# A rewritten prologue: four weight pieces on a second DMA queue, weight conversion begun earlier, one conversion tick a step

## The chip, the cores and the metric

The kernel runs on one core of one Trainium2 chip. The core has TensorE (PE, matmuls, with PEld for its weight loads), VectorE (DVE), ScalarE (ACT), GpSimd (POOL) and SyncE (SP), which here only issues DMAs. The metric is the device time of one execution in microseconds (us), lower is better. The time before is 1602.67 us, the median of three runs (1602.57 to 1602.93).

## The reference

Three stages follow one another on fp32 data: an attention through 32 memory slots for each of 8 batches and 8 heads of 576 rows, a two-layer network with a leaky ReLU, and a gated network.

```python
a   = softmax(phi, axis=m)                      # (B, H, S, 32)
k_m = einsum('bhsm,bhsd->bhmd', a, k);  v_m = einsum('bhsm,bhsd->bhmd', a, v)
x   = softmax(q @ k_m.T / sqrt(64)) @ v_m       # -> (4608, 512)
h   = x @ w_in;  x = maximum(0.01*h, h) @ w_out             # 512 -> 2048 -> 512
out = (sigmoid(x @ w_gate) * (x @ w_val)) @ w2_out          # 512 -> 1536 -> 512
```

The weights `w_in`, `w_out` and those of the gated network reach the kernel as 64-bit floats; the kernel reads them as pairs of 32-bit words and turns them into fp32 on the chip.

## The kernel before, in words

**Precision.** Every large matmul is done as three matmuls in a rounded fp32 format: high times high, low times high, high times low. `split` (L185) makes the high part with an ACT cast (L186) and the low part with a subtraction (L187) on DVE or POOL.

**Units.** A unit is one batch and one group of four heads; `units[0]` and `units[1]` are the two of batch 0. A unit goes through the parts `v1` to `v11` (vector work) and `t1` to `t8` (PE work): the softmax over phi (`v1`, `t1`, `v2`, `t2`, `v3`, exponential `v3e`, `v4`), the products with k and v (`t4`, into `ps_kv`), normalising and laying out (`v5r`, `v5x`, `t5`, `v6`), q transposed (`t7a`, `v7a`, `t7b`, `v7b`), scores (`t8a`, `v8a`, `t8b`, `v8b`), the second softmax (`v9`, `v9e`, `v10`), a transpose back (`v10t`) and the split into `at_hi` and `at_lo` (`v11`). In the text, `v9.1` is part v9 of unit 1. PSUM results of these parts share the two buffers of `ps_a`; the phi tile `ph` has one buffer, so that the load of unit 1's phi is issued after unit 0's `v3` has read it.

**Weight pieces.** `w_in` and `w_out` come in 32 pieces of 512 KB (class `Piece`, L197), two of each for every one of eight column blocks. `load` issues a DMA on SP's queue. The conversion of one piece has five stages: `a`, three ACT passes over 512 elements (L214, L215, L222); `b`, one DVE pass (L226); `b2`, one DVE pass (L234); `c`, one POOL pass (L242); `d`, for a `w_out` piece, a split into high and low part. `y`, the intermediate of `a`, `b` and `b2`, lies in SBUF. `tick()` (L1122) advances a pipeline by one: at tick n it emits `a` of piece n-1, `b` of n-2, `b2` of n-3, `c` of n-4, `d` of n-5; 37 ticks convert everything.

**Order.** Every engine works in program order, and so does SP's queue. The order is written out by hand. `SCHED['loads']` is the order of the loads on SP's queue: p, k and q of a unit number, or a count of weight pieces. `SCHED['prologue']` is a list of groups; in a group, the vector parts of each unit and the ticks (`T`) are interleaved by `run` (L1113), one instruction of each in turn, and then the PE parts follow. After the prologue, `first_vw` (L1176) multiplies v_m of batch 0 with a block of `w_in` (`vw_block`, L760), which gives `vw`.

**Main loop.** A step (L1254) takes 128 columns of the 2048 and half of a batch's 576 rows: `m1_in` (L801, 6 matmuls into `ps_h`, then leaky ReLU to `gr` and a split into `gh`, `gl`) runs two steps ahead; `m1_out` (L824) adds 12 matmuls into the four PSUM banks `acc`. Batch 0 has 32 steps in four groups of four columns for either half; when a group closes, the four banks are copied or added to `obuf` or `pbuf` (L844, L842), and the next group needs the banks again. In each of the first 30 steps `SCHED['ticks']` gives the number of ticks; `done_until` (L1151) adds ticks where a weight would be late, in `step_in` (L1171) and in `first_vw`. `SCHED['vw0']` are the steps at which the other six `vw` blocks are made. From step 32 on (batch 1) nothing of this remains.

Of the kernel before, what the change touches and what calls it, by code (L numbers as in the profile page):

```python
# [19 lines left out]

SCHED = {'vw0': [2, 5, 8, 13, 20, 22],
# [5 lines left out]
 'ticks': [1, 1, 1, 1, 2, 1, 1, 2, 0, 1, 0, 1, 1, 2, 0, 0, 0, 1, 1, 1, 1, 1, 0, 0, 1, 0, 0, 0, 0, 0],  # L27
 'lopool': [0, 1, 2, 3, 4, 5, 6, 7, 8, 9, 10, 11, 12, 13, 14],
 'gldve': [3, 4, 6, 12, 26, 31],
 'upool': ['v10.1', 'v10.2', 'v10.3', 'v11.0', 'v11.1', 'v11.2', 'v11.3', 'v9.0', 'v9.2', 'v9.3'],  # L30
 'chain': {'lp': -8,
# [64 lines left out]
            'lq3': 2,  # L96
            'v1': -5,
            't1': -1,
            'v2': 0,
            't2': 1,  # L100
            'v3': 3,
# [17 lines left out]
def tile_kernel(  # L119
# [77 lines left out]
    class Piece:  # L197
        late = False

        def __init__(self, src, done, f_dst=None, raw=None):  # L200
            self.src, self.done, self.f_dst, self.raw = src, done, f_dst, raw

        def load(self):
            self.raw = self.raw() if self.raw else cvp.tile([P, 2 * PC], U32, tag="raw", name="raw", bufs=2)
            r = self.raw
            if len(self.src.shape) == 3:
                r = r.rearrange("p (c f) -> p c f", c=self.src.shape[1])
            nc.sync.dma_start(out=r, in_=self.src)

        def a(self):  # L210
            w = self.raw.rearrange("p (n t) -> p n t", t=2)
            self.y = cvp.tile([P, PC], F32, tag="y", name="y", bufs=5)
            self.k = cvp.tile([P, PC], F32, tag="k", name="k", bufs=4)
            nc.scalar.activation(self.y, w[:, :, 1].bitcast(F32), AF.Abs, scale=2.0 ** -3)  # L214
            nc.scalar.activation(self.k, w[:, :, 0], AF.Copy, scale=2.0 ** -27, bias=2.0 ** 25)  # L215
            if not self.late:
                self.sign()
            yield
# [12 lines left out]
        def b2(self):  # L231
            w = self.raw.rearrange("p (n t) -> p n t", t=2)
            yi = self.y.bitcast(I32)
            nc.vector.scalar_tensor_tensor(  # L234
                out=yi, in0=yi, scalar=3, in1=w[:, :, 1].bitcast(I32),
                op0=ALU.logical_shift_left, op1=ALU.bitwise_xor,
            )
            yield
# [317 lines left out]
    def v5r(u):  # L556
# [6 lines left out]
        yield  # L563
        if u[0] == 0:
            nc.vector.tensor_scalar_mul(r, mask, r[:, 0:1])
            yield

    def v5x(u):
        s = un[u]
        p, r = s.pop("p"), s["r"]  # L570
        x = etile(u)
        x = s["x"] = x.rearrange("p a m -> p (a m)")[:, 0:4 * D].rearrange("p (a f) -> p a f", a=2)
# [103 lines left out]
    def v9m(u):  # L676
        s = un[u]
        nb = S // 32
        st = s["st"] = ap_.tile([P, nb], F32, tag="st", name="st", bufs=2)
        nc.vector.reduce_max(st, s["sc"], axis=AX.X)  # L680
        yield
# [406 lines left out]
    with tc.manual_schedule():  # L1088
# [10 lines left out]
        for j in range(NVB):  # L1099
            pieces += win_pieces(j) + wout_pieces(j)  # L1100
        n_start = len(pieces)

        raws = iter(pieces)

        def load_raws(n):
            for _ in range(n):
                p = next(raws, None)
                if p:
                    p.load()

# [59 lines left out]

        def step_in(b, hf, fc):  # L1171
            if (b, hf) == (0, 0):
                done_until(2 * (fc - fc % 2) + 4)
            return m1_in(b, hf, fc)

        def first_vw(j):  # L1176
            done_until(4 * j + 2)
            return vw_block(j)
# [15 lines left out]
        for x in SCHED["loads"]:  # L1194
            if isinstance(x, int):
                load_raws(x)
            elif "." in x:
                unit_qh(units[int(x[1])], int(x[3]))
# [5 lines left out]
        for group in SCHED["prologue"]:  # L1204
            vs, ts_ = {}, []
            for n, f in enumerate(waiting):
                vs["w", n] = [f()]
            waiting = []
            for x in group.split():
# [4 lines left out]
                else:  # L1214
# [4 lines left out]
                    else:  # L1219
                        ts_.append((PARTS[n], u))  # L1220
            run([chain(v) for v in vs.values()])
            for t in ts_:
# [9 lines left out]
        for i in range(LA):  # L1232
            fin = step_in(*steps[i])
            if i + 1 < LA:
                fin()
# [18 lines left out]
        for i, (b, hf, fc) in enumerate(steps):  # L1254
# [3 lines left out]
            if i + LA < len(steps):  # L1258
                fin = step_in(*steps[i + LA])
            else:  # L1260
# [22 lines left out]
            for n in {b, b + 1} - {0}:  # L1283
                if i in VW_AT.get(n, []):
                    vw_pair(n, 2 * VW_AT[n].index(i))
            m1_out(b, hf, fc)
            for f, u in ls:
# [71 lines left out]
```

## Time and profile before

| | us |
|---|---|
| median of 3 runs | 1602.67 |
| profiled execution, its own time | 1601.75 |
| span of its trace, first to last instruction | 1599.9 |
| PE busy (share of the span) | 1549.1 (97%) |
| ACT / DVE / POOL busy | 707.9 / 827.7 / 431.0 |

The profile describes one execution, 0.9 us below the median; 1.85 us of its time lie outside the span. Start times are counted from the first instruction. A row of the timeline gives start, duration, engine, line, operation, the tiles (out<-in) with their shapes, a count where neighbours were merged, and in brackets the idle time of that engine just before with what ended it. PEclk is the granted clock of TensorE as a share of 2.4 GHz; 0.50 is its lower level.

### The profile page before, as it was taken

What the parts mean: (1) busy time and instruction counts of PE and PEld (TensorE: products, weight loads), DVE (VectorE), ACT (ScalarE), POOL (GpSimd) and SP (SyncE); (2) the same over time, 40 slices, a digit from 0 to 9 for tenths busy, and PEclk for the clock granted to TensorE, in tenths of its full rate; (3) what the DMA queues carried; (4) which work ended last, traced back from release to release, by engine and by line L of the source; (5) the groups of instructions that cost most, each with busy time, mean ns of one, the idle gap of its engine ahead of it and who ended that gap; (6) DMA issues with size and microseconds to landing.
All of it is one profiled execution on the core that took longest, in us unless ns stands there. A gap on an engine that the chain in (4) does not pass through costs nothing.

```text
span 1599.9 us, 27447 instructions
## 1 busy us (share of the span) xinstructions
PE 1549.1 (97%) x10544; PEld 1358.0 (85%) x10544; DVE 827.7 (52%) x1426; ACT 707.9 (44%) x1602; POOL 431.0 (27%) x429
## 2 busy tenths in 40 slices
PE   5799999999999999999999999999999999999998
PEld 2677988999999998999988888888888888888898
DVE  6886444555554545422145474355545475255544
ACT  5885455565556555645333143223333143223332
POOL 3886343554445444543100020000200020000100
PEclk8799999999999999999999999999999999999999
DMA  9822554554556455322446446536546446536692
GB/s 306 277 53 64 160 143 138 150 154 139 159 146 192 140 160 146 115 82 97 146 170 218 140 156 234 191 115 222 195 163 222 141 150 236 169 109 223 223 398 76
DMA packets 203490, 268.66 MB, mean 168 GB/s; under 512 B 95072, under 2 KB 140128, under 8 KB 203360
## 3 DMA queue, kind: packets, MB, share of 16 engines
q1 hardware_dynamic: 203360, 266.92, 52.1%
q8 instruction: 83, 1.36, 0.4%
q14 instruction: 47, 0.39, 0.1%
HBM read 219.68 MB, written 47.19 MB: 167 GB/s over the span
## 4 chain that ended last, share of the span: by engine, by line
PE 82%; ACT 1%; DVE 1%; DMA 1%; issue 0%; POOL 0%; DVEq 0%; SPq 0%; ACTq 0%; POOLq 0%
PE acc L835 20%; PE oacc L1041 18%; PE ps_y L943 14%; PE ps_h L813 9%; PE ps_x L943 9%; PE ps_z L943 9%; PE ps_vw L783 1%; PE ps_kv L550 1%; DMA wt<-gvs 1%; PE ps_sc L625 0%; ACT gr L818 0%; ACT obuf L844 0%; DVE vw L795 0%; DVE t L530 0%; ACT raw L222 0%
## 5 line engine op out<-in xcount | busy, mean ns | idle before, releaser
L835 PE MATMUL acc<-gh,wo 128*128 128x288 f32 x2048 | 428.7, 301 | 3.7 <-ACT obuf L844 2.7
L835 PEld LDWEIGHTS acc<-gh,wo 128*128 128x128 f32 x2048 | 328.9, 189 | 28.4 <-issue 13.8
L835 PE MATMUL acc<-gl,wo 128*128 128x288 f32 x1024 | 304.8, 298 | 2.1 <-POOL gl L187 2.1
L187 POOL TENSOR_TENSOR gl<-gr,gh 128x288 fp32r<-128x288 f32 x250 | 215.6, 864 | 329.9 <-ACT gh L186 216.6
L1041 PE MATMUL oacc<-w2t,pt 128*128 128x512 f32 x1296 | 296.3, 389 | 0.0
L1041 PEld LDWEIGHTS oacc<-w2t,pt 128*128 128x128 f32 x1296 | 243.1, 188 | 50.3
L943 PE MATMUL ps_y<-xo,wt 128*128 128x512 f32 (+1 forms) x1080 | 251.9, 369 | 0.0
L813 PE MATMUL ps_h<-at_hi,vw 128*128 128x288 f32 x1024 | 214.6, 298 | 6.1 <-ACT vw L186 4.7
L943 PEld LDWEIGHTS ps_y<-xo,wt 128*128 128x128 f32 x1080 | 190.4, 188 | 33.8
L818 ACT ACTIVATE gr<-ps_h 128x288 f32<-128x288 f32 x256 | 105.7, 413 | 254.2 <-PE ps_h L813 226.1
L906 POOL TENSOR_TENSOR xo<-xr,xo 128x512 fp32r<-128x512 f32 (+1 forms) x16 | 23.0, 1460 | 671.0 <-ACT xo L902 671.0
L835 PEld LDWEIGHTS acc<-gl,wo 128*128 128x128 f32 x1024 | 193.7, 189 | 3.0 <-POOL gl L187 3.0
L813 PEld LDWEIGHTS ps_h<-at_hi,vw 128*128 128x128 f32 x1024 | 166.6, 190 | 7.5 <-ACT vw L186 5.6
L943 PE MATMUL ps_z<-xo,wt 128*128 128x512 f32 (+1 forms) x720 | 167.4, 368 | 0.6 <-DMA wt<-gvs 0.6
L943 PE MATMUL ps_x<-xo,wt 128*128 128x512 f32 (+1 forms) x720 | 167.5, 368 | 0.0
L813 PE MATMUL ps_h<-at_lo,vw 128*128 128x288 f32 x512 | 151.6, 296 | 0.0
L978 ACT CAST pt<-sg 128x512 fp32r<-128x512 f32 (+1 forms) x120 | 69.4, 578 | 182.0 <-DVE sg L971 182.0
L943 PEld LDWEIGHTS ps_z<-xo,wt 128*128 128x128 f32 x720 | 127.0, 189 | 23.1 <-DVE tmp L1024 0.7
L943 PEld LDWEIGHTS ps_x<-xo,wt 128*128 128x128 f32 x720 | 127.2, 188 | 22.9
L186 ACT CAST gh<-gr 128x288 fp32r<-128x288 f32 x256 | 111.8, 437 | 2.2
L813 PEld LDWEIGHTS ps_h<-at_lo,vw 128*128 128x128 f32 x512 | 97.2, 190 | 0.0
L990 ACT COPY tmp<-ps_x 128x512 f32<-128x512 f32 (+1 forms) x60 | 32.5, 542 | 136.6 <-PE ps_x L943 136.6
(171 smaller groups left out, 1719.0 us busy)
## 6 DMA issues: line engine op xcount, KB each, us to landing
wt<-gvs SPq DMA_DIRECT2D x210, 512.0 KB, 4.6
w2t<-w2s SPq DMA_DIRECT2D x60, 512.0 KB, 5.5
gvs<-hl SPq DMA_DIRECT2D x84, 256.0 KB, 2.4
x2s<-obuf SPq DMA_DIRECT2D x15, 576.0 KB, 3.7
win<-in_moe_w_in_dram SPq DMA_DIRECT2D x16, 512.0 KB, 9.8
wo_bits<-in_moe_w_out_dram SPq DMA_DIRECT2D x16, 512.0 KB, 10.4
xr<-x2s SPq DMA_DIRECT2D x16, 512.0 KB, 6.2
out_dram<-osum SPq DMA_DIRECT2D x32, 256.0 KB, 2.0
```

The lines of the kernel that those rows point to most:

```text
L186: nc.scalar.copy(hi, raw)
L187: eng.tensor_sub(lo, raw, f32(hi))
L550: nc.tensor.matmul(p[M * h:M * h + M, 0:2 * D], a, x, start=(c == 0), stop=(c == CC))
L783: nc.tensor.matmul(ps[g][M * h:M * h + M, n * VB:(n + 1) * VB], kvT[b, g][D * g:D * g + D, 1, M * h:M * h + M], win[j][D * g:D * g + D, h, ...
L813: nc.tensor.matmul(p[:, :HALF], w, x, start=(n == 0), stop=(n == 3 * NG - 1))
L818: nc.scalar.activation(gr, p[:, :HALF], AF.Prelu, alpha=0.01)
L835: nc.tensor.matmul(a[d][:, :HALF], w[:, ds_], x, start=(open_ and n == 0), stop=(close and n == 2),)
L906: eng.tensor_sub(t[:, 1, :h], x_operand(n, k, a), f32(t[:, 0, :h]))
L943: nc.tensor.matmul(bank, w[:, l, a, :], x[:, r, :h], start=(start and i == 0), stop=(i == 5), skip_group_check=not start,)
L978: nc.scalar.copy(d[:, 0, :h], s)
L990: read(lambda: nc.scalar.copy(s1, x))
L1041: nc.tensor.matmul(bank[i], pt[2 * f + t][:, l, q * P:(q + 1) * P], w2t[f][:, r, :], start=(f == 0 and l + r == 0), stop=(f == TH - 1 and ...
```

## The change

The first four weight pieces (`a4`) are issued on ACT's queue, ahead of everything else that ACT does; on SP's queue unit 0's and unit 1's k now come before their q, and the pieces that stood between them go behind unit 1's q. The prologue's groups are rewritten: the second tick, the first that converts anything, stands with `v3e.0`; both prologues have 12 ticks. `W` in a group makes the first two `vw` blocks inside the prologue, and their `waiting` splits come after the other vector work of the next group. `v1` of unit 2 moves from the prologue to step 0, and its `t1`, `v2`, `t2` one step on. The loop's ticks become one a step at most but for one step, two `vw` blocks come two steps later and one four, one one step later, and `done_until` moves from `m1_in` to `m1_out` with a later due time. The first nine pieces keep `y` between `a` and `b2` in a PSUM bank of the `acc` pool. `r` times `mask` (L565) goes from DVE to ACT. `v10.0` goes from DVE to POOL and `v10.1` from POOL to DVE; the row maxima and sums of unit 1 lie in a PSUM bank of `ps_h`.

```diff
@@ -18,16 +18,17 @@
 
 
 
-SCHED = {'vw0': [2, 5, 8, 13, 20, 22],
- 'loads': ['p0', 'q0', 'k0', 1, 'p1', 1, 'k1', 'q1', 2, 'p2', 16, 'k2', 32, 'q2.0', 'q2.1', 'q2.2', 'q2.3'],
- 'prologue': ['v1.0', 't1.0', 'v2.0 t7a.0 t2.0', 'v7a.0 v3.0', 'v3e.0 v4.0', 't7b.0 v1.1', 'T t4.0 t1.1', 'T',
-              'v5.0', 'v7b.0', 'v2.1', 't5.0', 'v6.0 t2.1 t8a.0', 'T v3.1', 'v3e.1 v8a.0 t8b.0', 't7a.1', 'v8b.0',
-              'v9.0 v7a.1 T v4.1 v9e.0 t4.1', 't7b.1 T', 't5.1 v5.1 v7b.1', 'T v1.2', 'v10.0 T', 't8a.1 v6.1',
-              'v10t.0 t8b.1 T v8a.1', 'v11.0', 'v8b.1 v9.1 T', 'T T v9e.1 T v10.1 v10t.1 v11.1'],
- 'ticks': [1, 1, 1, 1, 2, 1, 1, 2, 0, 1, 0, 1, 1, 2, 0, 0, 0, 1, 1, 1, 1, 1, 0, 0, 1, 0, 0, 0, 0, 0],
+SCHED = {'vw0': [4, 6, 12, 14, 20, 22],
+ 'loads': ['a4', 'p0', 'k0', 'q0', 'p1', 'k1', 'q1', 16, 'p2', 'k2', 32, 'q2.0', 'q2.1', 'q2.2', 'q2.3'],
+ 'prologue': ['T v1.0', 't1.0', 'v2.0 t2.0', 'v3.0 t7a.0', 'v3e.0 T v7a.0 v4.0 t4.0 t7b.0', 'T v7b.0 v1.1 t1.1',
+              'v5.0 v2.1 t5.0 t2.1', 'v6.0 T v3.1 t8a.0', 'v3e.1 T v8a.0 t8b.0 t7a.1',
+              'v8b.0 v7a.1 v4.1 T t4.1 t7b.1', 'v9.0 v7b.1 T', 'v5.1 v9e.0 T t5.1', 'v6.1 T t8a.1 W',
+              'v8a.1 v10.0 t8b.1', 'v8b.1 v9.1 T', 'v9e.1 T v10t.0 v11.0', 'v10.1 T W', 'v10t.1 v11.1'],
+ 'ticks': [1, 1, 1, 1, 1, 1, 1, 1, 0, 1, 1, 1, 1, 1, 1, 0, 1, 1, 1, 1, 1, 2, 1, 0, 1, 1, 1, 0, 0, 0],
+ 'banks': 9,
  'lopool': [0, 1, 2, 3, 4, 5, 6, 7, 8, 9, 10, 11, 12, 13, 14],
  'gldve': [3, 4, 6, 12, 26, 31],
- 'upool': ['v10.1', 'v10.2', 'v10.3', 'v11.0', 'v11.1', 'v11.2', 'v11.3', 'v9.0', 'v9.2', 'v9.3'],
+ 'upool': ['v10.0', 'v10.2', 'v10.3', 'v11.0', 'v11.1', 'v11.2', 'v11.3', 'v9.0', 'v9.2', 'v9.3'],
  'chain': {'lp': -8,
            'lk': -5,
            'lq0': -8,
@@ -94,10 +95,10 @@
             'lq1': 0,
             'lq2': 1,
             'lq3': 2,
-            'v1': -5,
-            't1': -1,
-            'v2': 0,
-            't2': 1,
+            'v1': -1,
+            't1': 0,
+            'v2': 1,
+            't2': 2,
             'v3': 3,
             'v3e': 3,
             'v4': 4,
@@ -195,21 +196,24 @@
     PC = 512
 
     class Piece:
-        late = False
+        late = bank = False
 
         def __init__(self, src, done, f_dst=None, raw=None):
             self.src, self.done, self.f_dst, self.raw = src, done, f_dst, raw
 
-        def load(self):
+        def load(self, eng=nc.sync):
             self.raw = self.raw() if self.raw else cvp.tile([P, 2 * PC], U32, tag="raw", name="raw", bufs=2)
             r = self.raw
             if len(self.src.shape) == 3:
                 r = r.rearrange("p (c f) -> p c f", c=self.src.shape[1])
-            nc.sync.dma_start(out=r, in_=self.src)
+            eng.dma_start(out=r, in_=self.src)
 
         def a(self):
             w = self.raw.rearrange("p (n t) -> p n t", t=2)
-            self.y = cvp.tile([P, PC], F32, tag="y", name="y", bufs=5)
+            if self.bank:
+                self.y = ps_acc.tile([P, PC], F32, tag="acc", name="y_bank")
+            else:
+                self.y = cvp.tile([P, PC], F32, tag="y", name="y", bufs=5)
             self.k = cvp.tile([P, PC], F32, tag="k", name="k", bufs=4)
             nc.scalar.activation(self.y, w[:, :, 1].bitcast(F32), AF.Abs, scale=2.0 ** -3)
             nc.scalar.activation(self.k, w[:, :, 0], AF.Copy, scale=2.0 ** -27, bias=2.0 ** 25)
@@ -230,9 +234,11 @@
 
         def b2(self):
             w = self.raw.rearrange("p (n t) -> p n t", t=2)
-            yi = self.y.bitcast(I32)
+            y = self.y
+            if self.bank:
+                self.y = cvp.tile([P, PC], F32, tag="y", name="y", bufs=5)
             nc.vector.scalar_tensor_tensor(
-                out=yi, in0=yi, scalar=3, in1=w[:, :, 1].bitcast(I32),
+                out=self.y.bitcast(I32), in0=y.bitcast(I32), scalar=3, in1=w[:, :, 1].bitcast(I32),
                 op0=ALU.logical_shift_left, op1=ALU.bitwise_xor,
             )
             yield
@@ -561,13 +567,13 @@
         yield
         nc.vector.reciprocal(r[:, 0:1], r[:, 0:1])
         yield
+
+    def v5x(u):
+        s = un[u]
+        p, r = s.pop("p"), s["r"]
         if u[0] == 0:
-            nc.vector.tensor_scalar_mul(r, mask, r[:, 0:1])
-            yield
-
-    def v5x(u):
-        s = un[u]
-        p, r = s.pop("p"), s["r"]
+            r = ap_.tile([P, 4], F32, tag="r", name="r", bufs=2)
+            nc.scalar.activation(r, mask, AF.Copy, scale=s["r"][:, 0:1])
         x = etile(u)
         x = s["x"] = x.rearrange("p a m -> p (a m)")[:, 0:4 * D].rearrange("p (a f) -> p a f", a=2)
         if u[0] == 0:
@@ -676,7 +682,10 @@
     def v9m(u):
         s = un[u]
         nb = S // 32
-        st = s["st"] = ap_.tile([P, nb], F32, tag="st", name="st", bufs=2)
+        if u == FIRST2:
+            st = s["st"] = ps_h.tile([P, 512], F32, tag="h", name="st_bank")[:, :nb]
+        else:
+            st = s["st"] = ap_.tile([P, nb], F32, tag="st", name="st", bufs=2)
         nc.vector.reduce_max(st, s["sc"], axis=AX.X)
         yield
 
@@ -1099,14 +1108,16 @@
         for j in range(NVB):
             pieces += win_pieces(j) + wout_pieces(j)
         n_start = len(pieces)
+        for p in pieces[:SCHED["banks"]]:
+            p.bank = True
 
         raws = iter(pieces)
 
-        def load_raws(n):
+        def load_raws(n, eng=nc.sync):
             for _ in range(n):
                 p = next(raws, None)
                 if p:
-                    p.load()
+                    p.load(eng)
 
         STAGES = ((1, "a"), (4, "c"), (2, "b"), (3, "b2"), (5, "d"))
 
@@ -1168,13 +1179,9 @@
         steps += [(b, hf, fc) for b in range(1, B) for hf in range(2) for fc in range(NF)]
         LA = 2
 
-        def step_in(b, hf, fc):
-            if (b, hf) == (0, 0):
-                done_until(2 * (fc - fc % 2) + 4)
-            return m1_in(b, hf, fc)
-
         def first_vw(j):
-            done_until(4 * j + 2)
+            while pos[0] < 4 * j + 6:
+                run([tick()])
             return vw_block(j)
 
         def unit_parts(i):
@@ -1194,6 +1201,8 @@
         for x in SCHED["loads"]:
             if isinstance(x, int):
                 load_raws(x)
+            elif x[0] == "a":
+                load_raws(int(x[1:]), nc.scalar)
             elif "." in x:
                 unit_qh(units[int(x[1])], int(x[3]))
             else:
@@ -1203,9 +1212,6 @@
         fin = None
         for group in SCHED["prologue"]:
             vs, ts_ = {}, []
-            for n, f in enumerate(waiting):
-                vs["w", n] = [f()]
-            waiting = []
             for x in group.split():
                 if x == "T":
                     vs.setdefault("T", []).append(tick())
@@ -1218,6 +1224,9 @@
                         vs.setdefault(u, []).append(PARTS[n](u))
                     else:
                         ts_.append((PARTS[n], u))
+            for n, f in enumerate(waiting):
+                vs["w", n] = [f()]
+            waiting = []
             run([chain(v) for v in vs.values()])
             for t in ts_:
                 if t:
@@ -1230,7 +1239,7 @@
             run([first_vw(n_vw)()])
             n_vw += 1
         for i in range(LA):
-            fin = step_in(*steps[i])
+            fin = m1_in(*steps[i])
             if i + 1 < LA:
                 fin()
 
@@ -1256,7 +1265,7 @@
                 fin()
                 fin = None
             if i + LA < len(steps):
-                fin = step_in(*steps[i + LA])
+                fin = m1_in(*steps[i + LA])
             else:
                 if not tmps:
                     tmp_open()
@@ -1283,6 +1292,8 @@
             for n in {b, b + 1} - {0}:
                 if i in VW_AT.get(n, []):
                     vw_pair(n, 2 * VW_AT[n].index(i))
+            if b == 0:
+                done_until(4 * (fc // 2) + 3 + fc % 2)
             m1_out(b, hf, fc)
             for f, u in ls:
                 f(u)
```

## Rows read from the trace of the kernel before

**Rows 1.** The page's part 1, busy time, share of the span, instructions.
```profile
PE 1549.1 (97%) x10544; PEld 1358.0 (85%) x10544; DVE 827.7 (52%) x1426; ACT 707.9 (44%) x1602; POOL 431.0 (27%) x429
```

**Rows 2.** Busy time by stretch; last three columns: PEclk, DMA share, GB/s.
```profile
0.00:5.00 5.00, 0.00 (x0) 0.00 (x0) 1.70 (x9) 1.28 (x1) 0.70 (x6) 1.00 0.49 119
5.00:10.00 5.00, 3.45 (x11) 1.98 (x11) 2.27 (x6) 1.42 (x3) 0.00 (x0) 1.00 0.96 250
...
25.00:50.00 25.00, 9.42 (x66) 3.27 (x58) 24.76 (x39) 20.38 (x41) 17.59 (x15) 0.64 1.05 381
...
70.00:80.00 10.00, 9.80 (x60) 8.47 (x61) 9.24 (x11) 9.74 (x23) 8.73 (x7) 0.69 0.32 63
...
110.00:120.00 10.00, 8.79 (x62) 8.33 (x63) 9.09 (x16) 7.38 (x17) 9.92 (x10) 1.00 0.10 28
...
140.00:200.00 60.00, 59.35 (x589) 54.31 (x576) 30.90 (x70) 28.78 (x77) 25.41 (x28) 1.00 0.43 122
```

**Rows 3.** Timeline of PE in the prologue.
```profile
8.85 1.08 PE L644 MATMUL ps_qT<-ident,q 128*128 128x128 f32 x4 [1.06 <-DVE pht L518]
11.88 1.94 PE L550 MATMUL ps_kv<-kv,e 128*32 128x128 f32 x32 [1.94 <-issue]
...
14.32 0.59 PE L552 MATMUL ps_kv<-ones,t 128*128 128x2 f32 x2
...
33.43 1.23 PE L661 MATMUL ps_sc<-qT,kvT 128*64 128x288 f32 x4 [2.97 <-ACT kvT L607]
...
36.20 1.94 PE L764 MATMUL ps_vw<-win,kvT 128*32 128x256 f32 x16
...
50.79 0.61 PE L813 MATMUL ps_h<-at_hi,vw 128*128 128x288 f32 x1 [4.72 <-ACT vw L186]
```

**Rows 4.** Timeline of ACT in the prologue and the first steps.
```profile
16.54 0.52 ACT L575 ACTIVATE e<-ps_kv,r 128x64 f32<-128x64 f32 x2 [1.30 <-DVE r L565]
...
53.70 0.41 ACT L818 ACTIVATE gr<-ps_h 128x288 f32<-128x288 f32 x1 [2.48 <-PE ps_h L813]
...
55.98 0.68 ACT L214 ACTIVATE y<-wo_bits 128x512 f32<-128x512 f32 x1
56.55 0.67 ACT L215 ACTIVATE k<-wo_bits 128x512 f32<-128x512 uint32 x1
...
69.77 1.28 ACT L844 COPY obuf<-acc 128x288 f32<-128x288 f32 x4
```

**Rows 5.** DVE's groups, shapes apart, 0 to 55 us: count, busy us, mean ns.
```profile
L226 DVE TENSOR_SCALAR y<-y 128x512 f32<-128x512 f32 x11 | 8.8, 799 | 0.0
L234 DVE SCALAR_TENSOR_TENSOR y<-y,win 128x512 int32<-128x512 int32 x6 | 6.4, 1060 | 0.0
...
L565 DVE TENSOR_SCALAR r<-mask,r 128x4 f32<-128x4 f32 x2 | 1.1, 548 | 0.1
...
L530 DVE TENSOR_REDUCE t<-e 128x128 f32<-128x512 f32 x1 | 1.0, 1032 | 0.5 <-ACT e L523 0.5
L671 DVE STREAM_TRANSPOSE e<-ps_sc 128x288 f32<-128x288 f32 x2 | 1.0, 483 | 0.9 <-PE ps_sc L661 0.8
...
L687 DVE TENSOR_TENSOR unit_a<-unit_a,st 128x576 f32<-128x576 f32 x1 | 0.7, 747 | 0.0
...
L516 DVE TENSOR_TENSOR e<-ph,ps_m 128x512 f32<-128x512 f32 x1 | 0.7, 687 | 1.5 <-PE ps_m L501 1.5
...
L518 DVE TENSOR_TENSOR pht<-pht,ps_m 64x128 f32<-64x128 f32 x1 | 0.3, 274 | 0.0
```

**Rows 6.** Timeline of PE: a block of vw, and the first matmul of step 4.
```profile
61.28 1.19 PE L764 MATMUL ps_vw<-win,kvT 128*32 128x256 f32 x16
...
70.20 0.85 PE L835 MATMUL acc<-gh,wo 128*128 128x288 f32 x2 [2.73 <-ACT obuf L844]
```

**Rows 7.** PE's waits from 50 to 140 us: total, times, longest.
```profile
PE acc L835 <- ACT obuf L844: 2.7, 1, 2.7
PE acc L835 <- POOL gl L187: 2.1, 3, 1.1
```

More of the change, by code (lines that the diff above doesn't have):

```diff
@@ L563, in v5r @@
         yield
-        if u[0] == 0:
-            nc.vector.tensor_scalar_mul(r, mask, r[:, 0:1])
-            yield
     def v5x(u):
@@ L570, in v5x @@
         p, r = s.pop("p"), s["r"]
+        if u[0] == 0:
+            r = ap_.tile([P, 4], F32, tag="r", name="r", bufs=2)
+            nc.scalar.activation(r, mask, AF.Copy, scale=s["r"][:, 0:1])
         x = etile(u)
```

## The prediction, made before the change was run

> **What bounds the kernel now.** I read the page's part 1 first: PE is busy for 97% of the span [rows 1], so only time in which PE stands idle or slow can be won. The table by stretch says where that is. From 140 us on PE is busy 59.35 of 60 us [rows 2], and the edits touch batch 0 alone, whose 32 steps end near there. Before 50 us PE has almost nothing to do; the first matmul of the main loop starts at 50.79 us [rows 3]. So two places count: the prologue, judged by the first `gr`, at 53.70 us [rows 4], and the 32 steps behind it.
>
> In the prologue DVE is busy for 24.76 of the 25 us from 25 to 50, but only for 4 of the first 10 us, and ACT for 2.7 [rows 2]. That is the room which an earlier conversion could use. In the steps the list of PE's waits is short: the longest is 2.73 us on the copies into `obuf`, at step 4, and three on `gl` sum to 2.1 us [rows 6, 7]. Behind the long one PEclk is 0.69 for ten microseconds [rows 2]: (1 - 0.69) x 10 = 3.1 us of PE lost, more than the wait itself. The wait of 1.1 us that is the longest on `gl` [rows 7] falls between 100 and 120 us, and the stretch from 110 keeps 1.00 [rows 2].
>
> **The change part by part: the inputs.** Unit 0's phi, k and q are 0.29 + 1.15 + 0.58 = 2.0 MB, the four pieces 2.1 MB. Before, the pieces came behind; now they share the DMA engines with the inputs. In the first 5 us 0.6 MB moved; at the next stretch's 250 GB/s that is 2.4 us, so transfers start near 2.6 us, and from there the engines are already 0.96 busy [rows 2]. There is little idle DMA time to fill. All 4.1 MB at 315 GB/s, midway between 250 for the inputs' small packets and 381 for weights [rows 2], take 13.0 us: q0, now the last, lands at L = 15.6 us. Bounds: 10.7 if SP's queue is served first (2.0 MB at 250), 19 if everything moves at 250. I take the middle since both kinds of packet are in it.
>
> The Trainium skill's page "DMA: Bandwidth & Descriptors", section "Issuing engines are not separate DMA queues", speaks against this edit: DMAs of several engines interleave on the same 16 DMA engines, and a second issuer saves only issue time. By it L is the 15.6 of the sum; by a queue that left the inputs alone it would be 10.7. Only the run can tell, since before has one issuer.
>
> On ACT the four issues stand ahead of its table load and first exponential; ACT did 1.28 us of work in the first 5 us [rows 2], so they are hidden. On SP nothing is lost: p1 waits for `v3.0` as before.
>
> **The prologue's path.** From L on I follow what waits for what in the new groups. Instructions queued on one engine overlap: two ACT passes of 0.68 start 0.57 apart [rows 4], so I count 0.57 for an ACT pass over 512 elements, 1.71 for stage `a`, and 0.1 off DVE's rows: 0.6 for 512 elements with a PSUM operand (0.69), 0.4 for a transpose, 0.95 for the reduction, 0.65 for 576 elements [rows 5].
> (1) PE: the last q transpose 0.27 (a fourth of 1.08), `t4.0` 3.03 (11.88 to 14.91), `t7b.0` 1.08 [rows 3]: 4.38.
> (2) ACT copies q 0.57, `v5x.0` five short passes at 0.26 [rows 4], `t5.0` as four transposes 1.08, `v6.0` 0.35 (half a pass) and 0.27: 3.57.
> (3) DVE: `v3.1` 0.6 and 0.2, `v8a.0` and `v8b.0` 0.4 each, `v4.1` 0.95 and 0.27, three ticks at 1.2: 6.42.
> (4) the sums' matmuls 0.59, `t7b.1` 1.08, its copy 0.57, `a` 1.71, `v9e.0` 0.6, `a` 1.71, `v5x.1` 1.3: 7.56.
> (5) `t5.1` 1.08, `v6.1` 0.62, `t8a.1` 1.23, the block of vw 1.94 [rows 3]: 4.87.
> (6) its split 0.57 + 0.6, two small passes 0.54, `v8b.1` 0.4, `v9.1` 0.65 twice, a tick 1.2: 4.61.
> (7) `v9e.1` 0.6, `a` 1.71, two casts 0.7, `a` 1.71, a weight cast and a vw cast 1.14, `at_hi` 0.3, `at_lo` 0.8, the last matmul 0.5: 7.46.
> Together 38.9 us, so the first `gr` comes at 54.5 against 53.70: +0.8. The bounds of L make it -4.1 to +4.2.
>
> What is gained on this path is smaller than it looks. Two ticks more are done when `v5x.1` comes, but they stand ahead of it on ACT, and the first 15.6 us belong to the loads. The number of ticks before step 0 is 12 in both.
>
> **Ticks through PSUM.** Before, `b` and `b2` took 0.80 and 1.06 us on average, against 0.69 for a pass with one PSUM operand [rows 5]. No row shows either with `y` in PSUM. I take 0.69 (0.6 apart), the nearest row by shape; at the old prices the four ticks that stand on DVE's legs of the path cost 0.66 more each, +2.6; below, nothing shorter than 0.6 apart is to be seen.
>
> The skill's page "VectorE: DVE Perf Modes", section "Why PSUM operands drop a tier", weighs against it: fp32 with a PSUM operand runs at one element a cycle, so `b` can be slower than in SBUF with the engine to itself. This trace's mean of 0.80 in SBUF lies above 0.69 all the same; by the mean the edit wins 0.1 on `b`, and the rule's loss would show only where POOL is quiet.
>
> **Small moves.** `r` times `mask` leaves DVE (0.55 [rows 5]) for ACT (0.26, counted). `v10.0` on POOL and `v10.1` on DVE are one 576-element pass each way. `v1` of unit 2, 1.03 + 0.27 on DVE [rows 5], now falls in step 0, while PE works on the first `m1_in` at half clock: hidden; without that cover 1.3.
>
> **The steps.** The old `done_until` in `step_in` forces one tick at step 0 (12 done, 13 wanted), so steps 0 to 3 had five ticks; now four. The third vw block goes from step 2 to 4. Up to step 4 ACT thus does 1.71 + 0.57 less and reaches the `obuf` copies 2.28 sooner relative to the start of the steps; PE does a block of 1.19 less [rows 6] and is there 1.19 sooner. The wait shrinks by 1.1 to 1.6 us. Does the clock still fall? 1.6 is nearer to the 1.1 behind which it held than to the 2.73 behind which it fell, so I take no fall: -3.1. After step 8 three ticks more are left (pos 20 instead of 23): 17 in place of 14; POOL is full there (9.92 of 10 us [rows 2]), and its waits of 2.1 us grow in proportion: +0.45.
>
> **Sum.** +0.8 - 1.1 - 3.1 + 0.45 = -2.95. The profiled execution took 1601.75 us, a span of 1599.9 and 1.85 around it; it becomes 1598.8. On the median, 0.9 above it, 1599.7.
>
> **Rivals.**
> - *The clock falls all the same.* The loss of 3.1 stays: -2.95 + 3.1 = +0.15, 1602.8. For it: the gap is only cut, not closed. Against: 1.1 us did not trigger it.
> - *The backlog meets a later eviction.* Conversions put off to steps 9 to 26 stand on ACT, DVE and POOL where the banks must be emptied again (groups close at steps 7, 11, 15, ...). It decides when more than 2 us of queued work stand ahead of the copies; then a wait of 2.73 and a fall of 3.1 come there, on top of the one at step 4: +0.15 + 5.8 = +6.0, 1608.7, slower. For it: POOL at 9.92 and DVE at 9.09 of 10 us from 110 on. Against: the ticks are now spread one by one.
> - *SP's queue is served first.* L = 10.7 and the prologue wins 4.1: -4.1 - 1.1 - 3.1 + 0.45 = -7.85, 1594.8. For it: q0 stands in front of k0's products in PE's order, which pays only if it lands early. Against: the shared engines' 0.96.
> - *The change does nothing of note at the start*: `a` runs earlier, but the path waits for q0; this is within the forecast's +0.8.
>
> **Chances.** Forecast 0.38, clock falls 0.22, later eviction 0.20, inputs first 0.20. A measurement of this kernel tells 0.2%, 3.2 us, from no change. The forecast, with its own range of 1596.5 to 1602, lies half on either side of 1599.5: faster 0.20 + 0.19 + a little = 0.42; same 0.36; slower 0.22. The range of 1593 to 1607.5 leaves out the far ends of the last rival and of the slower one.
>
> **What would show it.** Right: the first product with q0 waits for a DMA until about 15 us; first `gr` near 54; `b` and `b2` near 0.69 each up to the ninth piece; PE's wait on `obuf` at step 4 under 2 us and PEclk 1.00 in the twenty microseconds after. Wrong: `gr` before 51 or after 57, a drop of PEclk behind any later eviction, or `b` above 0.8. I would be most wrong if the landing of q0 sets nothing because ACT is the later one.

## The result, and the profile after

The change made the kernel slower: 1620.5 us (median of 4 runs, 1619.5 to 1621.4) against 1602.6 beside it (4 runs, 1599.5 to 1602.9), a ratio of 1.0119 with a 95% interval of [1.0106, 1.0131]. The forecast was 1599.7 in a range of 1593 to 1607.5, so its sign is wrong and the time lies outside the range. The profiled execution of the changed kernel took 1621.35 us, 19.6 more than that of before. Three executions of the sets below were disturbed and stay out of every ratio: 6998 us (the loop alone), 2553 us (the step-4 wait taken away) and 8414 us (the kernel before).

Part 1 of the page of the changed kernel, to be held against [rows 1]:

```profile
PE 1555.0 (96%) x10544; PEld 1361.2 (84%) x10544; DVE 809.8 (50%) x1424; ACT 706.5 (44%) x1604; POOL 427.9 (26%) x429
```

PE is busy 5.9 us longer with the same 10544 matmuls, and stands idle for most of the rest; DVE, ACT and POOL are all busy for less time than before. Where the time went shows when the steps of batch 0 are laid side by side. Each entry is the start of the last `acc` matmul on `gl` in a step, read off PE's timeline in us:

| step | 0 | 4 | 5 | 8 | 11 | 13 | 14 | 17 | 18 | 21 | 22 | 31 |
|---|---|---|---|---|---|---|---|---|---|---|---|---|
| before | 57.6 | 73.0 | 78.0 | 89.1 | 98.1 | 105.6 | 108.2 | 116.7 | 120.2 | 132.4 | 136.9 | 164.9 |
| after | 59.9 | 71.8 | 74.2 | 86.5 | 94.7 | 101.5 | 112.5 | 121.0 | 129.8 | 141.6 | 154.7 | 182.7 |
| difference | +2.2 | -1.2 | -3.8 | -2.6 | -3.4 | -4.1 | +4.3 | +4.2 | +9.6 | +9.2 | +17.8 | +17.8 |

The changed kernel starts 2.2 us late, is 4.1 us ahead after step 13, and then loses 8.4, 5.4 and 8.6 us in three single steps: 14, 18 and 22. After step 22 nothing moves until the end of the batch, and 1.8 of the 19.6 us come later than step 31.

Timeline of PE in the changed kernel around these three steps (start, length, operation; in brackets the idle time before it and what ended it):

```profile
102.74 0.63 PE L773 MATMUL ps_vw<-win,kvT 128*32 128x256 f32 x4
107.84 1.92 PE L773 MATMUL ps_vw<-win,kvT 128*32 128x256 f32 x12 [4.48 <-POOL win L248]
...
123.27 0.40 PE L844 MATMUL acc<-gh,wo 128*128 128x288 f32 x1 [1.21 <-ACT wo L187]
127.25 0.61 PE L844 MATMUL acc<-gh,wo 128*128 128x288 f32 x1 [3.59 <-POOL wo L188]
...
136.44 1.07 PE L773 MATMUL ps_vw<-win,kvT 128*32 128x256 f32 x16
...
146.08 0.62 PE L773 MATMUL ps_vw<-win,kvT 128*32 128x256 f32 x4 [3.30 <-POOL win L248]
150.77 1.92 PE L773 MATMUL ps_vw<-win,kvT 128*32 128x256 f32 x12 [4.06 <-POOL win L248]
```

Two are `vw` blocks: the sixth block (index 5, step 14) gets through 4 of its 16 matmuls and then stands for 4.48 us until POOL has done the addition `c` on the second half of its `win` piece; the eighth (index 7, step 22) waits for both halves. The one between is the down projection of step 18 (`m1_out`), whose `wo` piece has only just been split on ACT and POOL. None of these waits stands in [rows 7]. Together they are 1.21 + 3.59 + 4.48 + 3.30 + 4.06 = 16.6 us of the 22.3 that the three steps lose.

Of the other 5.7 us about 1 is the sixth block itself, which stood in step 13 before. Most of what is left is the clock: 12 matmuls of a block take 1.92 us behind a wait, and all 16 of the block in step 20, with no wait ahead of it, take 1.07. Busy time by stretch of the changed kernel (length, then PE, PEld, DVE, ACT, POOL, PEclk, DMA share, GB/s), against [rows 2]:

```profile
25.00:50.00 25.00, 13.93 (x103) 5.92 (x102) 19.01 (x39) 19.84 (x41) 13.59 (x11) 0.76 1.06 379
70.00:80.00 10.00, 8.81 (x71) 6.91 (x64) 7.21 (x12) 9.17 (x21) 9.46 (x7) 1.00 0.30 60
...
110.00:120.00 10.00, 9.44 (x60) 9.19 (x60) 5.12 (x12) 4.54 (x10) 3.28 (x4) 0.86 0.01 2
...
140.00:200.00 60.00, 50.73 (x502) 43.69 (x500) 27.60 (x60) 28.59 (x70) 27.21 (x27) 0.94 0.29 79
```

And a finer cut of the first of the three waits:

```profile
100.00:105.00 5.00, 3.37 (x24) 2.56 (x22) 3.83 (x6) 4.76 (x10) 5.00 (x5) 1.00 0.01 2
105.00:108.00 3.00, 0.15 (x4) 0.16 (x8) 3.00 (x3) 1.64 (x4) 3.00 (x4) 0.67 0.00 0
108.00:112.00 4.00, 4.00 (x21) 2.72 (x18) 0.34 (x1) 0.00 (x0) 0.99 (x1) 0.50 0.02 4
112.00:116.00 4.00, 4.00 (x28) 3.98 (x28) 1.22 (x2) 1.22 (x3) 0.00 (x0) 0.89 0.00 0
```

While PE waits, POOL is full (3.00 of 3). Then PE resumes at a clock of 0.50, half speed, and now ACT (0.00 of 4 us) and POOL (0.99, then 0.00) have nothing, because what they are given next depends on PE's new products; ACT's next row shows it:

```profile
113.86 0.41 ACT L827 ACTIVATE gr<-ps_h 128x288 f32<-128x288 f32 x1 [7.22 <-PE ps_h L822]
```

So this wait of PE on POOL costs the wait and the slow matmuls behind it, and it leaves the converters idle. That their idle time makes the next pieces late as well is likely, but no run shows it apart. POOL was 9.92 of 10 us busy from 110 to 120 us before [rows 2]; now 3.28.

POOL's own timeline says why the addition of step 14 came so late:

```profile
100.58 0.81 POOL L188 TENSOR_TENSOR gl<-gr,gh 128x288 fp32r<-128x288 f32 x1
101.35 1.29 POOL L248 TENSOR_TENSOR win<-y,k 128x512 int32<-128x512 int32 x1
102.61 1.34 POOL L696 TENSOR_TENSOR e<-e,st 128x576 f32<-128x576 f32 x1
103.91 1.72 POOL L188 TENSOR_TENSOR wo<-y,wo 128x512 fp32r<-128x512 f32 x1
105.59 0.79 POOL L188 TENSOR_TENSOR gl<-gr,gh 128x288 fp32r<-128x288 f32 x1
106.35 1.44 POOL L248 TENSOR_TENSOR win<-y,k 128x512 int32<-128x512 int32 x1
```

PE reaches the block at 102.74 and needs the last of these rows. The three ahead of it (1.34, 1.72, 0.79) were queued earlier and POOL runs them in order without a gap. In the code, `c` of the block's second piece, number 4j+1, belongs to the tick that brings the count of ticks to 4j+6, and the new `first_vw` asks for exactly 4j+6 ticks. Counted through the two lists, the changed kernel has 26 ticks done at block 5 and 34 at block 7, which is 4j+6 to the tick: the addition is issued immediately ahead of the block that needs it. The list alone brings this about, since the new due times add no tick anywhere. The kernel before had 28 at block 5 (step 13) and 35 at block 7 (step 22); it reached 26 in step 12 and 34 in step 21, so that the addition was issued a step ahead of the block. (Of the six blocks one moved by two steps, one by four, and two by one, block 5 among these.)

Step 18 has lost slack too, but not all of it: its `w_out` piece is split in tick 28, which stood in step 13 before, five steps ahead, and stands in step 17 now, one step ahead. POOL takes 3.19 us for the addition in front of the split:

```profile
122.80 3.19 POOL L248 TENSOR_TENSOR y<-y,k 128x512 int32<-128x512 int32 x1
125.94 1.26 POOL L188 TENSOR_TENSOR wo<-y,wo 128x512 fp32r<-128x512 f32 x1
```

At step 22 POOL is not full. The list puts two ticks in step 21 and one in step 22, and they pass through ACT and POOL one behind the other:

```profile
143.43 1.36 POOL L188 TENSOR_TENSOR wo<-y,wo 128x512 fp32r<-128x512 f32 x1 [4.58 <-issue]
144.76 1.27 POOL L248 TENSOR_TENSOR win<-y,k 128x512 int32<-128x512 int32 x1
147.27 1.26 POOL L188 TENSOR_TENSOR wo<-y,wo 128x512 fp32r<-128x512 f32 x1 [1.24 <-ACT wo L187]
...
149.46 1.25 POOL L248 TENSOR_TENSOR win<-y,k 128x512 int32<-128x512 int32 x1
```
```profile
142.68 0.62 ACT L187 CAST wo<-y 128x512 fp32r<-128x512 f32 x1
144.83 0.67 ACT L218 ACTIVATE y<-wo_bits 128x512 f32<-128x512 f32 x1 [1.53 <-POOL wo L188]
```

POOL stands idle for 4.58 and 1.24 us ahead of the two splits, though PE needs the two `win` additions behind them. Each split starts just after ACT's cast of the same piece ends (the first at 143.30), and ACT's next conversion waits 1.53 us for POOL's first split.

The prologue, in the changed kernel's timelines of PE and ACT, against [rows 3] and [rows 4]:

```profile
14.59 2.15 PE L650 MATMUL ps_qT<-ident,q 128*128 128x128 f32 x4 [3.04 <-DMA q<-in_q_dram]
16.67 1.94 PE L556 MATMUL ps_kv<-kv,e 128*32 128x128 f32 x32
...
37.78 0.89 PE L601 MATMUL ps_kvT<-ident,unit_a 128*128 128x128 f32 x2 [5.28 <-ACT unit_a L581]
```
```profile
6.25 1.28 ACT L529 ACT_TABLE_LOAD   x1 [6.25 <-DMA win<-in_moe_w_in_dram]
...
54.22 0.43 ACT L187 CAST at_hi<-atr 128x288 fp32r<-128x288 f32 x1 [0.81 <-DVE atr L739]
55.84 0.41 ACT L827 ACTIVATE gr<-ps_h 128x288 f32<-128x288 f32 x1 [1.19 <-PE ps_h L822]
```

The first `gr` is at 55.84 against 53.70, +2.1 where +0.8 was forecast.

DVE's groups of the changed kernel from 0 to 55 us, against [rows 5]:

```profile
L230 DVE TENSOR_SCALAR y_bank<-y_bank 128x512 f32<-128x512 f32 x9 | 6.1, 682 | 0.0
L240 DVE SCALAR_TENSOR_TENSOR y<-y_bank,win 128x512 int32<-128x512 int32 x5 | 3.4, 678 | 0.0
...
L230 DVE TENSOR_SCALAR y<-y 128x512 f32<-128x512 f32 x1 | 0.4, 416 | 0.0
```

### The profile page after: what moved, and what is told of

Its sections match the earlier page's. It is cut to its first block, busy times and chain, and to the rows that moved or that the text cites. A ratio compares the mean times of both kernels' runs of the same rounds, so it can differ in the third digit from the quotient of the medians.

```text
span 1619.6 us, 27441 instructions
## 1 busy us (share of the span) xinstructions
PE 1555.0 (96%) x10544; PEld 1361.2 (84%) x10544; DVE 809.8 (50%) x1424; ACT 706.5 (44%) x1604; POOL 427.9 (26%) x429
## 4 chain that ended last, share of the span: by engine, by line
PE 79%; DMA 2%; ACT 2%; DVE 1%; issue 1%; SPq 0%; POOL 0%; DVEq 0%; ACTq 0%; POOLq 0%
PE oacc L1050 18%; PE acc L844 18%; PE ps_y L952 14%; PE ps_x L952 9%; PE ps_z L952 9%; PE ps_h L822 8%; PE ps_vw L792 1%; PE ps_kv L556 1%; DMA kv<-in_k_dram 1%; DMA wt<-gvs 1%; PE ps_sc L631 0%; DMA ph<-in_phi_dram 0%; ACT gr L827 0%; DVE vw L804 0%; DMA raw<-in_moe_w_gate_dram 0%
```

## The experiments

Four kernels split the change in two and try the due times. The new loop (tick list, `vw0`, due times) is called the loop; all else is the start.

**The loop undone.** The changed kernel with the loop of before:

```diff
- 'vw0': [4, 6, 12, 14, 20, 22], 'ticks': [1, 1, 1, 1, 1, 1, 1, 1, 0, 1, 1, ...
+ 'vw0': [2, 5, 8, 13, 20, 22],  'ticks': [1, 1, 1, 1, 2, 1, 1, 2, 0, 1, 0, ...
-            while pos[0] < 4 * j + 6:
-                run([tick()])
+            done_until(4 * j + 2)
-            if b == 0:
-                done_until(4 * (fc // 2) + 3 + fc % 2)
```
(and `step_in` as before)

> The changed kernel with the loop's part of the edit undone: ticks, the steps of the vw blocks and both due times as before; the new loads, the new prologue and the PSUM banks stay. Theory A (the loss is made in the loop: vw blocks and w_out pieces are used as soon as their last conversion stage is emitted, and PE waits for POOL): the first gr stays near 55.8 us, the waits of PE on the converted win of 4.5, 3.3 and 4.1 us go, and the time is 1602.6 + 2, within 1601 to 1607. Theory B (the prologue, the second queue or the banks cost it): the time stays above 1614.

Measured: 1605.1 us (1603.4 to 1606.0), ratio to before 1.0017 [1.0008, 1.0026]. The three waits are gone; on `win` 2.0 us in all are left, and PEclk is 1.00 from 80 to 200 us. So the loop holds about 15.5 of the change's 18 us, and the start costs the remaining 2 to 3.

**The loop alone**, the kernel before with the new loop:

> The kernel before with the loop's part of the edit alone: one tick a step, the vw blocks' new steps and the new due times; prologue, loads, banks as before. Theory A: PE waits on POOL's win before the blocks of steps 14 and 22, three microseconds or more each, PEclk falls behind them, and the time is 1614 to 1622. Theory B: no more than 1606.

Measured: 1618.6 us, ratio 1.0099 [1.0082, 1.0116], so +16 us without any edit to the start. One more execution of the same kernel gives the trace:

> The kernel before with the new loop alone (ticks, vw0, due times), to see its waits. Theory A (the due times leave no slack, whatever the prologue): PE waits over 3 us on POOL's win at vw blocks 5 and 7 (steps 14 and 22) and on wo near step 18, the granted clock under 0.9 in the stretches behind them, step 31 ends near 180 us against 164.9; time 1616 to 1620. Rival (the waits of the changed kernel come from its later prologue): none of these waits over 2 us, and the loss is spread over other places.

Measured: 1616.75 us. PE's waits from 50 to 190 us (total, times, longest), and the stretches from 100 to 160:

```profile
PE ps_vw L764 <- POOL win L242: 9.9, 3, 3.6
...
PE acc L835 <- POOL wo L187: 3.6, 1, 3.6
PE acc L835 <- ACT wo L186: 1.2, 1, 1.2
```
```profile
100.00:110.00 10.00, 5.86 (x34) 3.53 (x33) 6.97 (x8) 5.05 (x11) 6.41 (x6) 0.79 0.00 1
...
120.00:130.00 10.00, 5.16 (x26) 4.71 (x25) 7.32 (x10) 5.60 (x12) 9.52 (x7) 0.83 0.08 24
130.00:140.00 10.00, 10.00 (x120) 8.63 (x119) 4.91 (x12) 7.16 (x15) 5.71 (x6) 1.00 0.33 57
140.00:160.00 20.00, 11.92 (x78) 8.36 (x78) 6.51 (x15) 6.33 (x15) 8.09 (x7) 0.74 0.23 56
```

The same three places, the same kind of wait (block 5's was 2.99, a little under the 3 expected), the clock down behind each. The late start of the changed kernel is not their cause. The last `gl` matmul of step 31 starts at 181.3.

**One tick in each of the first 25 steps**, on the changed kernel:

```diff
- 'ticks': [1, 1, 1, 1, 1, 1, 1, 1, 0, 1, 1, 1, 1, 1, 1, 0, 1, ...
+ 'ticks': [1, 1, 1, 1, 1, 1, 1, 1, 1, 1, 1, 1, 1, 1, 1, 1, 1, ...
```

> The changed kernel with the ticks of the loop put earlier: one in each of the first 25 steps, so that one tick more is done at step 14 and one more at step 22; all else as changed. Theory A (what lacks is time between the last conversion stage and its use): one step of PE work, 2.4 us, then stands between them; the waits on win fall below 2 us, PEclk stays up, and the time is 1598 to 1604. Theory C (POOL as a whole is too full for these conversions wherever they stand): the waits move to other steps and the time stays above 1612.

Measured: 1608.7 us, ratio 1.0041 [1.0026, 1.0056]. That is 12 us of the 15.5, but 5 above what was expected. The waits on `win` are gone; in their place stand others:

```profile
PE acc L844 <- POOL gl L188: 4.3, 1, 4.3
PE ps_vw L773 <- DVE e L641: 3.1, 1, 3.1
```

So the rule "the due time has no slack" explains the size of the loss, and not that all of it can be had back by pulling ticks forward. The wait on `gl` is at step 18, where two ticks more are done than in the changed kernel, and POOL runs without a gap for 9 us before it. The other is at block 4 (step 12, one tick more): DVE is late with a pass that frees a PSUM buffer. That the earlier ticks are what makes both late is argued; no run took them apart.

**One tick more asked for ahead of each block**, on the changed kernel:

```diff
-            while pos[0] < 4 * j + 6:
+            while pos[0] < 4 * j + 7:
```

> The changed kernel with the due time of a vw block one tick later (4j+7 instead of 4j+6 ticks done), as it was before; ticks, steps and all else as changed. The tick that this forces is emitted in the same step, straight ahead of the block. Theory A, which counts PE's work between conversion and use and not ticks: it does not help, the waits at steps 14 and 22 stay or grow, 1617 to 1626. Rival D (a distance of one more tick in the pipeline is enough, since the product's last stage then is one tick old): under 1610.

Measured: 1614.7 us, ratio 1.0077 [1.0062, 1.0092], between the expectations. Step 22 now waits 3.08 instead of 3.30 + 4.06; step 14 still 4.49:

```profile
108.89 1.92 PE L773 MATMUL ps_vw<-win,kvT 128*32 128x256 f32 x12 [4.49 <-POOL win L248]
...
145.21 1.92 PE L773 MATMUL ps_vw<-win,kvT 128*32 128x256 f32 x12 [3.08 <-POOL win L248]
```

A tick forced at the block itself comes too late to help that block: POOL's queue is as long as before. It helps later blocks, because the count stays one ahead: block 7 has its tick 34 a step earlier, and 7.36 us of waits become 3.08. So slack counts as steps of PE's work that lie between the addition and the block, and one step is not always enough.

Four more kernels take the start apart and test what the wait at step 4 is worth.

**The loads undone too**: the loop undone, and the order of loads as before.

> e1_loop_undone with the order of the loads as before: no piece on the second queue, q0 ahead of k0, the first four pieces between the units' loads. The prologue's order and the banks stay as changed. Theory P (the 2.1 MB beside them delay unit 0's inputs, and that is the prologue's 3 us): q0's products start near 7 us instead of 14.5, k0's near 12 instead of 16.7, the first gr comes 3 to 5 us earlier than in e1 (56.7), near 52 to 54, and the time is 1599 to 1602. Rival Q (the new order on ACT and DVE sets the end whatever lands when): gr stays within 1 us of 56.7 and the time near 1605.

Measured: 1602.3 us, ratio 1.0005 [0.9997, 1.0014]. The products with q0 and k0 move as expected (6.88 and 11.91), the first `gr` only from 56.66 to 54.70, less than the 3 to 5 us expected. About 2 us of the start go with the loads. The size is rough: the intervals of the two kernels overlap, and the first `gr` of one and the same prologue differs by up to 0.9 us from trace to trace (see below).

**The banks undone**: the loop undone, and `'banks': 0`.

> e1_loop_undone without PSUM banks for the conversion (y of all pieces in SBUF). If the banks spare DVE its waits for POOL, b and b2 of the first nine pieces return from about 0.68 each to 0.8 and 1.06 on average; the prediction priced that at 2.6 us on the path, so the first gr comes at 57 to 59.5 and the time is 1605 to 1608. If ACT and the loads set the path, gr stays within 0.5 us and the time within 1 us of e1.

Measured: 1606.8 us, ratio 1.0033 [1.0021, 1.0046]; first `gr` 58.48 instead of 56.66; `b` 0.70 and `b2` 1.02 and 1.19 us on average instead of 0.68 each. By the first `gr` the banks are worth about 1.8 us.

**The step-4 wait taken away from the kernel before**, by itself:

```diff
-SCHED = {'vw0': [2, 5, 8, 13, 20, 22],
+SCHED = {'vw0': [4, 6, 8, 13, 20, 22],
- 'ticks': [1, 1, 1, 1, 2, 1, 1, 2, 0, ...
+ 'ticks': [1, 1, 1, 1, 2, 1, 2, 2, 0, ...
-            if (b, hf) == (0, 0):
+            if (b, hf) == (0, 0) and fc >= 4:
                 done_until(2 * (fc - fc % 2) + 4)
```

> The kernel before with the third and fourth vw blocks at steps 4 and 6 instead of 2 and 5, no forced tick at step 0 and the tick that this saves at step 6; all else as before. In the changed kernel PE's wait of 2.73 us on obuf at step 4 is gone, since the block of vw stands there and fills it, and PEclk stays at 1.00. If that is what these two moves give, it can be had alone: the wait goes, PEclk in 70 to 80 us is above 0.95, and the time is 1596 to 1599.5. If the wait has only moved (to the obuf or pbuf copies of a later group), 1601 to 1604.

Measured: 1605.3 us, ratio 1.0020 [1.0011, 1.0030]: slower, where 3 to 6 us were expected as a gain. The wait of 2.73 at step 4 is gone, and step 5 ends at 71.3 us instead of 78.0. By step 7 the lead of 6.7 us has vanished (84.4 against 84.5), and step 8 is 4.6 behind (93.7 against 89.1). PE in between:

```profile
74.73 0.40 PE L813 MATMUL ps_h<-at_hi,vw 128*128 128x288 f32 x1 [3.11 <-ACT vw L186]
...
86.34 0.40 PE L813 MATMUL ps_h<-at_hi,vw 128*128 128x288 f32 x1 [1.61 <-ACT vw L186]
87.55 0.61 PE L813 MATMUL ps_h<-at_hi,vw 128*128 128x288 f32 x1 [0.81 <-DVE vw L187]
```

The block moved from step 2 to step 4 (66.38 us on PE) serves the columns of step 8, whose `m1_in` PE reaches in step 6. By then ACT is inside a run of ticks: from 68.86 to 74.08 us it does conversions, an exponential and one `gr`, and only then the cast of `vw`. PE had been waiting since 71.6. The next block, made at step 6, is late in the same way for `m1_in` of step 10. The gap has moved two steps down, and PEclk falls there instead (0.84 from 70 to 90 us).

**All three together**: the start with the old loads, and this loop.

> The new prologue and banks with the loads as before (e5) and the loop of e7. If the gains of e5 and e7 are apart in time and add, it is as fast as e7 or 1 to 2 us faster, 1595 to 1599; if the new order of the prologue is itself worse than the old one, it is slower than e7 by that much.

Measured: 1604.9 us, ratio 1.0022 [1.0013, 1.0031], again a miss: 3.9 us of waits on ACT's `vw` have come, and 2.29 on `win` at block 5, whose addition is a step ahead as in the kernel before.

**The banks alone**, on the kernel before. If the banks were the one part that pays, they should beat both kernels without the rest:

```diff
+ 'banks': 9,
-            self.y = cvp.tile([P, PC], F32, tag="y", name="y", bufs=5)
+            if self.bank:
+                self.y = ps_acc.tile([P, PC], F32, tag="acc", name="y_bank")
+            else:
+                self.y = cvp.tile([P, PC], F32, tag="y", name="y", bufs=5)
```
(and `b2` writing to SBUF, as in the change)

> The kernel before with one part of the change alone: the first nine pieces keep y in a PSUM bank between a and b2; loads, groups and loop as before. Theory P+ (the banks are the useful part, and the rewritten groups and the loads ate it): undoing the banks moved the first gr from 56.66 to 58.48 us, so here it moves from 53.70 to about 51.9, b and b2 at 0.68 each, and the loop, paced by ACT and POOL, keeps about half to all of it: 1600.0 to 1601.7, 0.1 to 1.6 us under the kernel before. Rival (the loop gives all back, because its steps wait for conversions that come when they came before): 1602.0 to 1603.

Measured: 1600.0 us (1598.4 to 1600.6, 11 runs) against 1601.4 beside it (15 runs), ratio 0.9988 [0.9979, 0.9997]. This is the fastest kernel of the study. The gain is small, 0.12%, and the upper end of its interval lies only just below 1. Timeline of ACT:

```profile
51.90 0.41 ACT L824 ACTIVATE gr<-ps_h 128x288 f32<-128x288 f32 x1 [1.89 <-PE ps_h L819]
```

1.80 us sooner than before, as expected, and step 31 ends 1.8 sooner too (163.1 against 164.9): this loop gives nothing back.

## Why the prediction was wrong

**The step that failed** is the last term of the part on the steps: "After step 8 three ticks more are left (pos 20 instead of 23): 17 in place of 14; POOL is full there ..., and its waits of 2.1 us grow in proportion: +0.45." It asked how many ticks remain, and scaled the waits on `gl`. It never asked when each piece is due. The changed `first_vw` was in the diff, and so were the two lists: adding them up gives 26 and 34 ticks at blocks 5 and 7 against a need of 26 and 34. The runs put +16 us (the loop alone) in the place of the loop's three terms, -1.1 - 3.1 + 0.45, and in that kernel the waits on late pieces are 9.9 + 3.6 + 1.2 = 14.7 us. A price for step 14 could also have been had from before: a POOL that is full [rows 2] runs its queue in order, so an addition issued right in front of the block comes after several passes of 0.8 to 1.7 us. For step 22 this would not have served, since POOL had idle time there and the ticks waited for one another.

**The slower rival** had the right direction and the wrong place. "The backlog meets a later eviction" expected one wait of 2.73 and one fall of the clock, on `obuf`. Three came, of 4.5 to 7.4 us, on `win` and `wo`, and none over 0.6 us on an eviction of `acc`. Its chance of 0.20 and price of +6.0 were low because of it.

**The wait at step 4, -1.1, and the clock behind it, -3.1.** The forecast that the clock would hold there came true: PEclk is 1.00 from 70 to 80 us. The wait went altogether, because the block moved to step 4 fills it. But neither term was money in the bank. Taking this wait away from the kernel before made it about 3 us slower. And with the old loop the time from the first `gr` to step 31 does not follow the clock. It is 111.45 us with the loop undone, where PEclk is 0.83 from 70 to 80 us, 111.42 with the loads undone as well, where it is 1.00, and 111.17 in the kernel before, where it is 0.69. PE with the loads undone, at step 4 and at the block behind it:

```profile
71.40 0.53 PE L844 MATMUL acc<-gh,wo 128*128 128x288 f32 x2 [1.82 <-ACT obuf L853]
...
75.47 1.06 PE L773 MATMUL ps_vw<-win,kvT 128*32 128x256 f32 x12 [0.83 <-POOL win L248]
```

This kernel starts step 4 1.2 us later than the one before (70.20 [rows 6]), goes on at full clock, and then waits 0.83 us for POOL; the last `gl` matmul of step 5 starts at 78.02 in it and at 78.03 in the kernel before. POOL set the pace there, and PE at half clock merely arrived when its operand did. (This is shown for these steps alone: behind step 31 the trace with the loads undone, at a mean clock of 0.999 against 0.989, is 2.1 us shorter.) I had priced the slow clock as lost time without asking what PE would have waited for at full clock.

**The prologue, +0.8.** Mis-sized: +2.1 at the first `gr`, +2 to 3 us on the total. Its parts, by the first `gr` of four kernels, are: banks -1.80 (53.70 to 51.90), the rewritten groups and small moves +2.80 (51.90 to 54.70), the loads +1.96 (54.70 to 56.66). The 0.8 us from there to the changed kernel's 55.84 are scatter: four kernels with the same code up to this point have 55.84, 56.66, 56.33 and 56.73, so each part is known to about a microsecond.
- The loads were forecast well. The first products with q0 wait until 14.59 and end near 16.7, for an L of 15.6; before, with q0 ahead of k0 and no pieces beside it, they started at 5.41. The Trainium skill, "DMA: Bandwidth & Descriptors", section "Issuing engines are not separate DMA queues", says that transfers issued by several engines interleave on the same 16 DMA engines; the trace agrees in that q0 landed well behind the 10.7 that a queue left to itself would give, and the rival by which SP's queue is served first is out.
- The groups were where the sum was short, and in its last part. As I wrote, the two ticks more stand ahead of `v5x.1` on ACT: it runs at 37.2 us, and PE's `t5.1` behind it has waited 5.28 us. But the sum has that, with 37.5 for `t5.1` against 37.78. From `t5.1` to the first `gr` it has 16.9 us, and 18.1 were measured. It counts the conversions ahead of ACT's last `at_hi`, but not that this cast then waits 0.81 us for a transpose on DVE (the row at 54.22), which stands behind the low half of the `vw` split there. In the banks-alone kernel, with the old groups, `t5.1` starts at 30.81 after a wait of 2.11.
- The banks were forecast right: 0.68 for each pass, against 0.69. The Trainium skill, "VectorE: DVE Perf Modes", section "Why PSUM operands drop a tier", has an fp32 pass with a PSUM operand at one element a cycle; the trace agrees in that the one `b` left in SBUF took 0.42, against 0.68 in a bank. What decides here is the mean in SBUF: in the kernel before, from 20 to 155 us, the passes in SBUF that ran while POOL stood still took 0.38 to 0.42 us for `b` and 0.68 to 0.69 for `b2`, and those that took longer than 0.7 us, up to 1.53 and 1.78, all ran while POOL was at work for most of their time.

**What bounds the kernel.** That the prologue and the 32 steps hold everything was right: 17.8 of the 19.6 us are there. The 1.8 us after step 31 are within what this part varies by: from the last `gl` matmul of step 31 to the end of the span the traces take 1432.9 to 1436.9 us, the kernel before 1435.0 and the changed one the most, and the loop alone 1433.6. What is open is why pulling all ticks forward still leaves 3.7 us over the kernel with the loop undone. The waits that replace the old ones are named, but no run took them away.

## What to carry over

When work is put off, compare for each consumer the moment its last piece is issued with the moment it is needed, in steps of the consumer's work; averages of load, and counts of what is left, show nothing of a slack that has gone to zero. A wait of the main engine, or a low clock behind one, is only worth its length if the other engines could have delivered sooner: look at what is late next before it enters the sum. A change of many parts can hold one that pays; here nine PSUM buffers gave 0.12% while the schedule around them cost ten times that.

## What the chip showed that was not expected

- After each long wait on POOL PE went on at half the clock: 0.50 from 108 to 112 us behind 4.48 us, and still 0.89 from 112 to 116; two waits of 3.30 and 4.06 within nine microseconds kept 140 to 160 at 0.83 in the changed kernel, and 0.74 in the loop alone.
- `b2` on two SBUF operands beside a busy POOL takes 1.02 to 1.19 us on average, 0.68 with one operand in a PSUM bank. `b`, which the prediction feared to slow down, stayed nearly the same: 0.70 with the banks undone, 0.68 in a bank.
- The four issues on ACT's queue put its table load 6.25 us into the span, which cost nothing, since its first exponential ran at 12.31, after a wait of 4.78 us for DVE.
- PEclk can read 1.00 while matmuls still run at the low level's rate: with the loads undone two matmuls into `ps_h` took 0.68 us together from 55 to 57 us at a PEclk of 1.00, as from 52 to 54 us at 0.50 in the kernel before; at the full rate they take 0.43.
